# Register reads moved behind stores, two products moved inside a chain, one index tile split in five

## The chip, the cores and the metric

The kernel runs on one core of a Trainium2 chip, as one launch. The metric is the device time in microseconds (us) of that launch. TensorE (PE; its weight loads are shown apart as PEld) multiplies matrices, VectorE (DVE) and ScalarE (ACT) work elementwise, GpSimd (POOL) does elementwise work too and issues the indirect DMAs, SyncE (SP) issues most of the plain DMAs and reads numbers into registers. Each engine works through its own list in order; semaphores order the engines among themselves. 16 DMA engines move the data.

## What is computed

An attention block without softmax feeds a mixture of experts. With 8 batches, 8 heads, 576 positions and a head width of 64:

```python
kv = np.einsum('bhsd,bhse->bhde', k, v)
out = np.einsum('bhsd,bhde->bhse', q, kv)
rms = np.sqrt(np.mean(out * out, axis=-1, keepdims=True) + 1e-06)
x = (out / rms * g_norm)          # then (B,H,S,D) -> (4608, 512)

do_compute = x @ w_skip > 0
xc = x[do_compute]
logits = xc @ w_gate
e_idx = np.argmax(logits, axis=1)                      # 8 experts
probs = softmax(logits);  gate_w = probs[rows, e_idx]
for e in range(8):
    mask = e_idx == e
    h = np.maximum(xc[mask] @ w1[e], 0.0)              # 512 -> 1024
    y[mask] = gate_w[mask, None] * (h @ w2[e])         # 1024 -> 512
out = x.copy();  out[do_compute] = xc + y
```

Each token is 512 wide. A token with a score of zero or less keeps its x; every other one goes through the one expert that its logits choose.

## The kernel before

**Attention.** The 4608 tokens are worked in 36 units (`NU` = 36), two for each of 18 pairs of token tiles. A unit `n` runs in a loop over steps (L1034): `values(n)` on TensorE, `squares` on VectorE, `root` on ScalarE, `norm(n - 1)` on VectorE, then `weigh`, which puts the product with `g_norm` on a list `late`. `scale` works that list off; its job is `eng.tensor_tensor` at L628, on POOL unless an engine is named. A pair's x stands in a tile `xb` of two units; the pool `xb_pool` has six buffers, and pairs 2 to 5 stand in `room`, the space of a weight tile. When a pair's second product is issued, its two stores of 256 KB each (L670, or L659 for the last tile column of four batches, as in pair 17) are put down for the "end" part of a later step and issued by SP. All x is written to the output tensor `out` in DRAM; the experts' inputs are then gathered from there by row.

**The number chain.** For each group of token tiles `choose` finds the expert, `rank` counts on TensorE, and `number` (L724) turns ranks into slots on VectorE, in steps that are separated by `yield`: `pr` and `top`, `s_i`, `lo_i`, `hi_k` (the first four steps), then `oha_k`, a one-hot matrix, in pieces. `columns` (`hits` at L759, then `weighed` at L767) makes the other factor `bv`, and `place` (L779) multiplies both on TensorE so that each slot receives its token's row number. For the last group all of this runs at step `NU`, without a loop around it (L1054 to L1064). After `rank(LAST)` comes the whole of `number(LAST)`, then `columns`, and behind them `scale(NU, eng=nc.vector)`: the last two products, those of pair 17, on VectorE. POOL has taken the product ahead of them (L1059).

**SP's list.** `know_expert(r)` (L830) reads the number of the expert at place r into an SP register. For r = 1 to 7 this is put down for the "end" of step `NU - 1`. The stores of pairs 16 and 17 are put down for the "end" of step `NU + 1`, so they stand behind these reads.

**From rows to gathers.** Behind the loop, the first part of expert 0 (192 slots, gathered early) goes through layer 1 and layer 2 while the remaining rows are being found. After `place`, `add_pieces` adds the row numbers to `srow` (L837). `slot_rows` makes `rows` and `src`, the indices of whole pieces of 128 slots. Pieces that do not stand at a multiple of 128, or are shorter, need their rows moved over partitions. There are nine of these, in five runs of equal form, and `again_rows` makes `arows` and `asrc` for them: copies on ScalarE into `moved` (L1139), then two VectorE instructions a run (L1154, L1156). The first call makes two runs (`SOON = 2`), the second, after `first_1(range(6, 7))`, the other three. `first_1` is layer 1 on TensorE with its ReLU on ScalarE (L1201). Then `gather_all` issues the gathers of experts 0, 1 and 2 on POOL (L1171), each with `src` or `asrc` as its index. TensorE turns expert 0's two remaining pieces (L1180) as soon as they have landed, and the next load of weights (L341, L351) is tied to the last of these transposes.

The code of the last step, as it stands before:

```python
drain(choose(LAST))
scale(NU, chosen[-1], 2)
first_bv = weighed(known_at[0][:, :, :], 0, NE, row_k, 2, gat_pool, NE)
rank(LAST)
drain(number(LAST))
last_bv.append(columns(NE, NT - NE, colid_i, row_k, 2, gat_pool, NE))
scale(NU, eng=nc.vector)
```

Of the kernel before, what the change touches and what calls it, by code (L numbers as in the profile page):

```python
# [8 lines left out]
FP32 = mybir.dt.float32  # L9
BF16 = mybir.dt.bfloat16  # L10
I32 = mybir.dt.int32
# [6 lines left out]
def kernel(  # L18
# [43 lines left out]
    nc = tc.nc  # L62
    B, H, S, D = q.shape
    DM = H * D
    N = B * S
    P = 128
    C = S // 64
# [6 lines left out]
    E, F = moe_w1.shape[0], moe_w1.shape[2]  # L74
# [3 lines left out]
    FC = F // 128  # L78
# [17 lines left out]
    gat_pool = ctx.enter_context(tc.tile_pool(name="gat", bufs=1))  # L96
    ps_g = ctx.enter_context(tc.tile_pool(name="ps_g", bufs=1, space=bass.MemoryType.PSUM))
    attn = ctx.enter_context(ExitStack())
    kv_pool = attn.enter_context(tc.tile_pool(name="kv", bufs=3))
# [107 lines left out]
    for i in range(KVD):  # L207
        t = kvd_pool.tile([P, 2, 2, 2, PK], FP32, name=f"kvd{i}")
# [25 lines left out]
    for a in range(2):  # L234
        r = slice(a * 64, (a + 1) * 64)
        nc.vector.tensor_scalar(out=gw_b[r, :, a, :, :],
                                in0=wraw[r, :, :].rearrange("e n (u w) -> e u w n", u=2),
# [55 lines left out]
    runs = {}  # L293
    for r, off, m in sorted(res, key=lambda x: (x[0] > 0, x[1] < KEPT, x[0])):
        col = r * CK + off // P
# [18 lines left out]
    NRES = len(res)  # L314
# [110 lines left out]
    nq = 0  # L425
# [25 lines left out]
    def at(step, part, job):  # L451
        todo.setdefault((step, part), []).append(job)

    def jobs(step, part):
        for job in todo.pop((step, part), []):
            job()
# [161 lines left out]
    def weigh(n, xl):  # L618

        nq, b, i, u = units[n]  # L620
        if u == 0:
            if nq in IN_ROOM:
                x = room[:, IN_ROOM.index(nq) * 2 * DM:(IN_ROOM.index(nq) + 1) * 2 * DM]
                xbs[nq] = x.rearrange("p (r d) -> p r d", r=2)
            else:
                xbs[nq] = xb_pool.tile([P, 2, DM], FP32, tag="xb", name="xb")
        xb = xbs[nq]
        late.append((lambda eng: eng.tensor_tensor(  # L628
            out=xb[:, :, 4 * u * D:(4 * u + 4) * D].rearrange("p r (w x) -> p r w x", w=2),
            in0=xl[:, :, :, G:G + 2 * D] if i is None else  # L630
            xl[:, :, :, G:G + 2 * D].rearrange("p w r x -> p r w x"),
            in1=g_b[:, :, :].rearrange("p a d -> p (a d)").unsqueeze(1).unsqueeze(1)
                .to_broadcast([P, 2, 2, 2 * D]), op=ALU.mult), nq, u == 1 and (lambda: store_x(nq, b, i))))
# [7 lines left out]
    def scale(n, behind=None, keep=0, eng=None):  # L641

        while len(late) > keep:
            job, nq, store = late.pop(0)
            ins = job(eng or nc.gpsimd)
            if behind:
                tc.add_manual_dep(ins.ins, behind.ins.name, WAIT, reason="VectorE's port is free then")
            store = store() if store else None
            if store:
                at(max(min(n + 2, NU + 1), store_from.get(nq, 0)), "end", store)  # L650
# [73 lines left out]
    def number(g):  # L724

        t0, t1 = ([0] + ends)[g], ends[g]
        nt = t1 - t0
        ohb, rk = ohbs.pop(g), rks.pop(g)
        pr = gat_pool.tile([P, TG, E], FP32, tag="pr", name="pr")[:, 0:nt, :]
        nc.vector.tensor_tensor(out=pr, in0=rk[:, 0:nt, :], in1=ohb, op=ALU.mult)  # L730
        nc.vector.tensor_copy(out=top[:, :], in_=rk[:, nt, :])
        yield
        s_i = gat_pool.tile([P, TG], I32, tag="s_i", name="s_i")[:, 0:nt]
        with nc.allow_low_precision(reason="whole numbers"):
            nc.vector.tensor_reduce(out=s_i, in_=pr, axis=AX.X, op=ALU.add)
        yield
        lo_i = gat_pool.tile([P, TG], I32, tag="lo_i", name="lo_i")[:, 0:nt]
        nc.vector.tensor_single_scalar(out=lo_i, in_=s_i, scalar=127, op=ALU.bitwise_and)
        yield
        nc.vector.tensor_single_scalar(out=hi_k[:, t0:t1], in_=s_i, scalar=7,  # L740
                                       op=ALU.arith_shift_right)
        yield
        step = 2 if g < LAST else nt // 2
        for t in range(0, nt, step):
            nc.vector.tensor_tensor(out=oha_k[:, t0 + t:t0 + t + step, :],
                                    in0=row128_i[:, :].unsqueeze(1).to_broadcast([P, step, P]),
                                    in1=lo_i[:, t:t + step].unsqueeze(2).to_broadcast([P, step, P]),
                                    op=ALU.is_equal)
            yield

    def drain(pieces):
        for _ in pieces:
            pass
# [76 lines left out]
    def know_expert(r):  # L830
        experts_of.append(nc.values_load(
            order_i[0:1, r:r + 1], engines=(mybir.EngineType.SP,), min_val=0, max_val=E - 1,
            skip_runtime_bounds_check_because="a permutation of the experts"))
# [186 lines left out]
    streams, turned_ahead = [], []  # L1020
    now = [0]
    at(NU - 4, "pe", lambda: load_second(0, gathered[-1]))
    for r in range(1, E):
        at(NU - 1, "end", lambda r=r: know_expert(r))
    at(NU - 3, "early", lambda: first_in(0))
    at(NU - 2, "early", lambda: first_layer_1(range(1), slice(0, P)))
    at(NU - 2, "pe", lambda: first_in(1))
# [6 lines left out]
    for n in range(NU + 2):  # L1034
        now[0] = n
        if 1 <= n < NU - 1 and n + 1 not in turned_ahead:
            turn(n + 1)
        if 1 <= n < THIRD + 3 or n == NU:
            root(n - 1)
        jobs(n, "early")  # L1040
        if n < NU:
            values(n)
        jobs(n, "mid")
        if THIRD + 3 <= n < NU:
            squares(n)
        jobs(n, "summed")
        done = norm(n - 1) if 1 <= n <= NU else None
        if n < THIRD + 3:
            squares(n)
        jobs(n, "squared")  # L1050
        jobs(n, "pe")
        if done:
            done()
        if n == NU:  # L1054
            for pair, job in enumerate(last_x):
                job()
                first_hidden(pair)
            drain(choose(LAST))
            scale(NU, chosen[-1], 2)  # L1059
            first_bv = weighed(known_at[0][:, :, :], 0, NE, row_k, 2, gat_pool, NE)  # L1060
            rank(LAST)
            drain(number(LAST))
            last_bv.append(columns(NE, NT - NE, colid_i, row_k, 2, gat_pool, NE))
            scale(NU, eng=nc.vector)  # L1064
        jobs(n, "dve")

        if n in ends[:LAST]:
            streams.append((PACE[ends.index(n)], gating(ends.index(n))))
        for pace, stream in streams:
            for job in itertools.islice(stream, pace):  # L1070
                if job:
                    part, job = job if isinstance(job, tuple) else ("pe", job)
                    at(n + 1, part, job)
                    break
        jobs(n, "end")
    for _, stream in streams:
        assert next(stream, 0) == 0
    assert not todo
# [3 lines left out]
    with tc.tile_pool(name="wpool_b", bufs=1, reuse_waits="tile") as wpool_b, \  # L1082
# [60 lines left out]
        def again_rows(rows, src, which):  # L1143

            moved = gat_pool.tile([P, NRES], FP32, tag=f"moved{which.start}", name="moved")
            again_of(moved, srow, which)
            i = 0
            for j, ((_, m, _), cols) in enumerate(runs.items()):
                n = P // m
                cs = slice(i, i + len(cols))  # L1150
                i += len(cols)
                if j not in which:
                    continue
                nc.vector.tensor_scalar(out=rows[:, cs], in0=moved[:, cs], scalar1=float(n),  # L1154
                                        scalar2=part_of[m][:, 0:1], op0=ALU.mult, op1=ALU.add)
                nc.vector.scalar_tensor_tensor(out=src[:, cs], in0=rows[:, cs], scalar=N * n,  # L1156
                                               in1=rows[:, cs], op0=ALU.is_lt, op1=ALU.mult)


# [7 lines left out]
        whole = [[(c * P, P, r * CK + c, False) for c in range(CK)] for r in range(E)]  # L1167
        def gather_piece(xg, piece, src, asrc):
            off, m, col, aside = piece
            idx = asrc if aside else src  # L1170
            nc.gpsimd.indirect_dma_start(  # L1171
                out=x_of(xg, off, m), out_offset=None, in_=cut_rows(m)[:, :],
                in_offset=bass.IndirectOffsetOnAxis(ap=idx[:, col:col + 1], axis=0))

        def expert_in(xg, xt, piece):
            off, m = piece[0:2]
# [379 lines left out]
        def first_1(fs):  # L1556
            layer_1(0, xt_first, ht0, slice(0, KEPT), fs)
# [7 lines left out]
        add_pieces(srow[:, :], sp, 2)  # L1565
        y_more = layer_2(0, ht_of, first[1], None, range(IN))
        arows = gat_pool.tile([P, NRES], I32, tag="arows", name="arows")
        asrc = gat_pool.tile([P, NRES], I32, tag="asrc", name="asrc")
        again_rows(arows, asrc, range(0, SOON))
        rows, src = slot_rows(slice(0, NCOL), gat_pool, "")  # L1570
        first_1(range(6, 7))
        again_rows(arows, asrc, range(SOON, len(runs)))
        first_1(range(7, FC))
        for r in range(3):
            gather_all(r, plan, src, asrc)
        layer_2(0, ht_of, first[0], y, range(IN, FC))
# [78 lines left out]
```

## Time and profile before

| | us |
|---|---|
| median of 3 runs | 367.91 |
| lowest and highest run | 367.71, 371.33 |
| the profiled execution, its own time | 368.03 |
| its span from first to last instruction | 366.2 |
| PE busy | 349.9 (96% of the span) |
| DVE, ACT, POOL busy | 248.0, 147.6, 124.2 |

The profiled execution's time is 1.8 us above its span; this is what lies ahead of its first and behind its last recorded instruction. The granted TensorE clock was 0.993 of full speed over the span. DMA moved 81.70 MB, 223 GB/s in the mean.

The attention stage takes the first 108 us or so, with the DMA engines full from 20 to 80 us. From 140 us on eight experts run on a full TensorE. The change lies between the two. A row of a timeline is to be read as: start in us from the span's start, duration in us, engine, line, operation, what it writes and reads, how often, and in brackets the idle time of its engine ahead of it with what ended that. SPq and POOLq are an engine's sequencer, which issues DMAs and waits. "Issue" in a chain is time in which nothing shown was waited for.

### The profile page before, as it was taken

The numbers are of one execution on the slowest core, as the hardware profiler recorded it, in microseconds if no ns is written. First come the engines' busy times: TensorE is split into PE (matmuls) and PEld (weight loads), VectorE is DVE, ScalarE is ACT, GpSimd is POOL, SyncE is SP. The second block draws the span as 40 slices with busy tenths as digits, with TensorE's granted clock in tenths as the row PEclk, the third lists the DMA queues.
The fourth block names the chain that finished last, engine by engine and source line by source line (L and its number), as shares of the span: only waits on it lengthen the run. The fifth ranks groups of instructions, "written<-read, shape, count | busy, mean of one in ns | idle before, by whom it ended". The sixth has DMA issues, their size and how long they took to land.

```text
span 366.2 us, 9553 instructions
## 1 busy us (share of the span) xinstructions
PE 349.9 (96%) x3751; PEld 304.9 (83%) x3751; DVE 248.0 (68%) x630; ACT 147.6 (40%) x424; POOL 124.2 (34%) x201
## 2 busy tenths in 40 slices
PE   8979997999989999999999999999999999999993
PEld 4768886888878659599879988989988998989982
DVE  2646578678999653875937676786776776878831
ACT  2537675477775243335104402511431430431410
POOL 8037677567785072223032103303203203002002
PEclk9999999899999999999999999999999999999999
DMA  7999999999939659983536437465563762601001
GB/s 265 379 387 377 391 390 389 394 366 313 330 109 358 228 159 377 378 267 77 220 89 224 138 152 232 135 230 162 186 230 93 257 230 51 243 1 57 3 2 54
DMA packets 32808, 81.70 MB, mean 223 GB/s; under 512 B 3242, under 2 KB 3250, under 8 KB 32756
## 3 DMA queue, kind: packets, MB, share of 16 engines
q1 hardware_dynamic: 29264, 70.53, 54.3%
q0 software_dynamic: 3472, 10.48, 8.6%
q8 instruction: 31, 0.51, 0.6%
q14 instruction: 21, 0.17, 0.1%
q10 hardware_dynamic: 20, 0.02, 0.0%
HBM read 66.80 MB, written 14.48 MB: 222 GB/s over the span
## 4 chain that ended last, share of the span: by engine, by line
PE 74%; DMA 9%; issue 7%; DVE 3%; ACT 3%; POOL 2%; SPq 0%; POOLq 0%; DVEq 0%; ACTq 0%
PE bank L1279 45%; PE bank L1211 8%; PE o_ps L507 5%; DMA v<-in_v_dram 4%; PE sum_ps L387 4%; PE bank L1199 3%; PE q_ps L469 3%; DMA w<-in_moe_w_dram 2%; PE bank L1180 2%; DVE xl L554 1%; DMA out_dram<-xb 1%; DMA xg<-out_dram,src 1%; DMA xg<-out_dram,asrc 1%; DVE rs L531 1%; ACT qT L472 1%
## 5 line engine op out<-in xcount | busy, mean ns | idle before, releaser
L1289 ACT COPY p<-bank 128x128 f32<-128x128 f32 (+6 forms) x70 | 20.8, 297 | 96.3 <-PE bank L1279 88.8
L1279 PE MATMUL bank<-xt,w 128*128 128x128 f32 (+5 forms) x336 | 55.5, 288 | 0.0
L1410 POOL DMA_INDIRECT out_dram<-xg,rows x14 | 14.0, 997 | 117.6 <-DVE xg L1407 114.3
L1279 PEld LDWEIGHTS bank<-xt,w 128*128 128x128 f32 x336 | 47.0, 190 | 1.9 <-DVE bank L1283 1.4
L1283 DVE TENSOR_TENSOR bank<-bank,p 128x128 f32<-128x128 f32 (+6 forms) x70 | 23.6, 337 | 29.8 <-PE bank L1279 27.7
L628 POOL TENSOR_TENSOR xb<-xl,g_b 128x512 f32<-128x512 f32 x26 | 31.8, 1222 | 17.2 <-DVE rs L545 14.2
L1279 PE MATMUL bank<-xs,s 128*128 128x128 f32 (+5 forms) x224 | 36.7, 289 | 0.0
L507 PE MATMUL o_ps<-kvd,qT 128*128 128x146 f32 x240 | 35.7, 291 | 0.7 <-DVE xl L554 0.5
L507 PEld LDWEIGHTS o_ps<-kvd,qT 128*128 128x128 f32 x240 | 32.0, 192 | 1.6 <-DVE xl L554 1.1
L1279 PEld LDWEIGHTS bank<-xs,s 128*128 128x128 f32 x224 | 31.1, 190 | 1.0 <-ACT p L1289 0.8
L1211 PE MATMUL bank<-w,ht 128*32 128x128 f32 (+2 forms) x424 | 29.9, 313 | 0.0
L387 PE MATMUL sum_ps<-v,k 64*64 64x64 f32 x1152 | 24.4, 225 | 5.1 <-issue 4.4
L531 DVE TENSOR_REDUCE rs<-sq 128x8 f32<-128x512 f32 x36 | 24.5, 681 | 5.2 <-ACT sq L521 5.0
L387 PEld LDWEIGHTS sum_ps<-v,k 64*64 64x64 f32 x1152 | 20.2, 136 | 9.4 <-issue 6.4
L554 DVE TENSOR_TENSOR xl<-o_ps,rs 128x584 f32<-128x584 f32 x32 | 24.5, 767 | 3.9
L1211 PEld LDWEIGHTS bank<-w,ht 128*32 128x32 f32 (+2 forms) x424 | 18.2, 119 | 10.6 <-issue 7.2
L1279 PE MATMUL bank<-t,ht 128*128 128x256 f32 x112 | 27.0, 384 | 0.0
L1279 PE MATMUL bank<-w,ht 128*128 128x256 f32 x112 | 26.5, 380 | 0.0
L1171 POOL DMA_INDIRECT xg<-out_dram,src x14 | 14.5, 1034 | 33.4 <-DMA out_dram<-xg,rows 17.5
L1279 PE MATMUL bank<-t,hs 128*128 128x256 f32 x112 | 25.3, 379 | 0.0
L521 ACT ACTIVATE sq<-o_ps 128x512 f32<-128x512 f32 x34 | 20.3, 596 | 12.3 <-PE o_ps L507 10.0
L1279 PEld LDWEIGHTS bank<-t,ht 128*128 128x128 f32 x112 | 20.8, 190 | 3.9 <-issue 1.2
(217 smaller groups left out, 673.0 us busy)
## 6 DMA issues: line engine op xcount, KB each, us to landing
w<-in_moe_w_dram SPq DMA_DIRECT2D x16, 2048.0 KB, 10.5
k<-in_k_dram SPq DMA_DIRECT2D x32, 288.0 KB, 6.1
v<-in_v_dram SPq DMA_DIRECT2D x32, 288.0 KB, 6.1
q<-in_q_dram SPq DMA_DIRECT2D x32, 288.0 KB, 5.7
out_dram<-xb SPq DMA_DIRECT2D x25, 256.0 KB, 5.9
out_dram<-w SPq DMA_DIRECT2D x8, 256.0 KB, 4.7
out_dram<-xb POOLq DMA_DIRECT2D x3, 256.0 KB, 6.3
xg<-out_dram,src POOLq DMA_INDIRECT x16, 3.5
```

The lines of the kernel that those rows point to most:

```text
L387: nc.tensor.matmul(out=sum_ps[w * 64:(w + 1) * 64, a, u, :], lhsT=kt[r, 2 * u + w, c, :], rhs=vt[r, 2 * u + w, c, :], start=(c == 0), stop ...
L507: nc.tensor.matmul(out=ps[:, w, 0:2 * PK].rearrange("p (r k) -> p r k", r=2)[:, :, cols], lhsT=qT[:, w, a, :], rhs=kvds[b % KVD][:, w, :, ...
L521: nc.scalar.activation(out=sq[:, :, :, :], in_=heads(ps, G, G + 2 * D), func=ACT.Square)
L531: nc.vector.tensor_reduce(out=rs[:, :, :], in_=sq[:, :, :, :].rearrange("p x y (a d) -> p x (y a) d", a=2), axis=AX.X, op=ALU.add)
L554: nc.vector.tensor_tensor(out=xl[:, :, :, :].rearrange("p x y (a k) -> p x (y a) k", a=2), in0=ps[:, :, 0:2 * PK].rearrange("p x (h k) -> ...
L628: late.append((lambda eng: eng.tensor_tensor(out=xb[:, :, 4 * u * D:(4 * u + 4) * D].rearrange("p r (w x) -> p r w x", w=2), in0=xl[:, :, ...
L1171: nc.gpsimd.indirect_dma_start(out=x_of(xg, off, m), out_offset=None, in_=cut_rows(m)[:, :], in_offset=bass.IndirectOffsetOnAxis(ap=idx[:, ...
L1211: nc.tensor.matmul(out=yps[q * m:(q + 1) * m, 0:n], lhsT=ht(f)[:, off:off + m], rhs=w_sb[r][1][:, f, q * n:(q + 1) * n], start=(f == 0), s ...
L1279: nc.tensor.matmul(out=out, lhsT=lhsT(i), rhs=rhs(i), start=start and i == 0, stop=i == k - 1, skip_group_check=True)
L1283: nc.vector.tensor_tensor(out=to, in0=x, in1=y, op=ALU.add)
L1289: nc.scalar.copy(out=t, in_=x)
L1410: ins = nc.gpsimd.indirect_dma_start(out=cut_rows(m)[:, :], out_offset=bass.IndirectOffsetOnAxis(ap=rows[:, col:col + 1], axis=0), in_=x, ...
```

## The change

Four edits, all between the last steps of attention and the first gathers:

- `know_expert(1)` to `know_expert(7)` leave the "end" of step `NU - 1` and stand behind the whole loop, so behind all x stores on SP.
- The two products of pair 17 on VectorE leave their place behind `columns` and stand inside `number(LAST)`, behind `hi_k` and ahead of `oha_k`. Their output leaves `xb_pool` and takes a buffer of the pool that held K (three buffers in turn; this one was last used for batch 5).
- `asrc`, one tile of nine columns, becomes five tiles, one a run; each gather reads the column of its own run's tile.
- The second `again_rows` no longer stands between `first_1` of blocks 6 and 7 but ahead of both.

```diff
@@ weigh
                 xbs[nq] = x.rearrange("p (r d) -> p r d", r=2)
+            elif n >= NU - 2:
+                x = kv_pool.tile([P, 4, C, D], FP32, tag="k", name="k")
+                x = x[:, :, :, :].rearrange("p j c d -> p (j c d)")[:, 0:2 * DM]
+                xbs[nq] = x.rearrange("p (r d) -> p r d", r=2)
             else:
                 xbs[nq] = xb_pool.tile([P, 2, DM], FP32, tag="xb", name="xb")
@@ ahead of the loop
-    for r in range(1, E):
-        at(NU - 1, "end", lambda r=r: know_expert(r))
@@ step NU
             rank(LAST)
-            drain(number(LAST))
+            numbers = number(LAST)
+            for _ in range(4):
+                next(numbers)
+            scale(NU, eng=nc.vector)
+            drain(numbers)
             last_bv.append(columns(NE, NT - NE, colid_i, row_k, 2, gat_pool, NE))
-            scale(NU, eng=nc.vector)
@@ behind the loop
+    for r in range(1, E):
+        know_expert(r)
@@ again_rows
-                nc.vector.scalar_tensor_tensor(out=src[:, cs], in0=rows[:, cs], scalar=N * n,
+                nc.vector.scalar_tensor_tensor(out=src[j][:, :], in0=rows[:, cs], scalar=N * n,
                                                in1=rows[:, cs], op0=ALU.is_lt, op1=ALU.mult)
@@ gather_piece
-            idx = asrc if aside else src
+            at_row = asrc[col] if aside else src[:, col:col + 1]
             nc.gpsimd.indirect_dma_start(
                 out=x_of(xg, off, m), out_offset=None, in_=cut_rows(m)[:, :],
-                in_offset=bass.IndirectOffsetOnAxis(ap=idx[:, col:col + 1], axis=0))
+                in_offset=bass.IndirectOffsetOnAxis(ap=at_row, axis=0))
@@ ahead of the gathers
-        asrc = gat_pool.tile([P, NRES], I32, tag="asrc", name="asrc")
-        again_rows(arows, asrc, range(0, SOON))
+        asrcs = [gat_pool.tile([P, len(cols)], I32, tag=f"asrc{j}", name="asrc")
+                 for j, cols in enumerate(runs.values())]
+        asrc = [t[:, i:i + 1] for t, cols in zip(asrcs, runs.values()) for i in range(len(cols))]
+        again_rows(arows, asrcs, range(0, SOON))
         rows, src = slot_rows(slice(0, NCOL), gat_pool, "")
-        first_1(range(6, 7))
-        again_rows(arows, asrc, range(SOON, len(runs)))
-        first_1(range(7, FC))
+        again_rows(arows, asrcs, range(SOON, len(runs)))
+        first_1(range(6, FC))
```

## The prediction

> **What bounds the kernel now.** I read the head of the page first, then the busy times of each engine by stretch, then the chain of work that ended last, then the timeline of each engine between 115 and 136 us.
>
> ```profile
> PE 349.9 (96%) x3751; PEld 304.9 (83%) x3751; DVE 248.0 (68%) x630; ACT 147.6 (40%) x424; POOL 124.2 (34%) x201
> 131.50:133.40 1.90, 1.03 (x8) 0.66 (x9) 1.69 (x8) 0.59 (x1) 1.60 (x2) 1.00 0.38 71
> 140.00:150.00 10.00, 10.00 (x95) 7.78 (x97) 4.85 (x10) 5.48 (x22) 2.22 (x2) 1.00 1.03 385
> 240.00:366.00 126.00, 120.52 (x934) 110.25 (x932) 85.06 (x202) 34.13 (x101) 18.91 (x20) 0.99 0.37 127
> ```
>
> The last three rows are stretches: their length, then the busy time of PE, PEld, DVE, ACT and POOL, the granted clock, the DMA share and GB/s. TensorE is busy 96% of the span. In the expert stage it is simply full (10.00 of 10.00 us), so a microsecond saved ahead of 140 us reaches the end, and a microsecond saved on another engine inside that stage does not. The change touches only what happens between 116 and 134 us, and there one stretch is not full: 1.03 of 1.90 us. Whatever the change can bring is in these 0.87 us or close to them. The idle time in the last row lies at the end of the program, behind the last matmul, and moves with it.
>
> ```profile
> 119.46 3.60 PE L1211 MATMUL bank<-w,xg 128*128 128x512 f32 x8
> 122.90 0.51 PE L779 MATMUL g_ps<-bv,oha_k 128*128 128x48 bf16 x14
> 125.22 2.87 PE L1199 MATMUL bank<-xt_first,w 128*128 128x192 f32 x16
> 127.92 3.60 PE L1211 MATMUL bank<-w,ht 128*128 128x512 f32 x8
> 132.12 0.66 PE L1180 MATMUL bank<-ident,xg 128*128 128x128 f32 x4 [0.60 <-DMA xg<-out_dram,asrc]
> 133.04 0.33 PE L1180 MATMUL bank<-ident,xg 128*128 128x128 f32 x1 [0.27 <-DMA xg<-out_dram,asrc]
> 133.30 1.95 PE L1211 MATMUL bank<-w,ht 128*64 128x256 f32 x16
> ```
>
> The timeline of PE (start, duration, what, idle time before it and who ended it) shows the two gaps: 0.60 us and 0.27 us, each ended by the landing of a gather that reads its rows through `asrc`. They are the two pieces of expert 0 that are turned on TensorE at L1180. Every other instruction in this list starts where its predecessor ends. The chain says why these gathers are late:
>
> ```profile
> 123.70 4.17 DMA out_dram<-xb
> ...
> 128.75 1.00 POOL xg L1171
> 129.75 0.30 issue
> 130.06 2.94 DMA xg<-out_dram,asrc
> ```
>
> The last x store lands at 127.87 (123.70 + 4.17), the first gather starts at 128.75, the second at 130.06, and that lands at 133.00. The first gather has a second condition, which the timeline of POOL names:
>
> ```profile
> 128.75 1.00 POOL L1171 DMA_INDIRECT xg<-out_dram,asrc  x1 [10.82 <-DVE asrc L1156]
> 128.29 0.16 DVE L1156 SCALAR_TENSOR_TENSOR asrc<-arows 128x2 int32<-128x2 int32 x1
> DMA to landing us min/median/max: 2.9/3.1/3.3
> L1211 PE MATMUL bank<-w,ht 128*128 128x512 f32 x8 | 3.6, 592 | 0.0
> ```
>
> It waits for an index write that ends at 128.45, 0.58 us behind the last store. So two conditions end almost together, and both must move before the gather can. (The third line is the issue-to-landing time of the two gathers; the fourth, of the groups by form, gives the 592 ns of one of the eight matmuls from 127.92, which the sum uses.)
>
> **The change, part by part.**
>
> *Expert numbers behind the stores.* The timeline of the SP queue and the one line that groups the seven reads:
>
> ```profile
> 117.28 1.72 SPq L670 DMA_DIRECT2D out_dram<-xb  x2
> L831 SPq TENSOR_LOAD <-order_i x7: 262/273/530, 119.0 to 121.4; - x7
> 121.78 1.11 SPq L670 DMA_DIRECT2D out_dram<-xb  x2
> 123.02 1.50 SPq L659 DMA_DIRECT2D out_dram<-xb  x2
> 133.40 0.40 SPq L341 DMA_DIRECT2D w<-in_moe_w_dram  x1
> ```
>
> SP issues the stores of pair 15, then reads seven numbers from 119.0 to about 121.7, then issues the stores of pairs 16 and 17. The reads leave that place: 121.78 − 119.00 = 2.8 us. Pair 16's last product is POOL's, done at 117.80 (next fence), so its two stores can be issued from 119.0 and end near 120.15 (1.11 us). The reads now stand behind pair 17's stores, and the next thing behind them on SP is the weight load of expert 1, which goes out behind the transposes, at 133.40; seven reads of about 0.3 us from 121.7 end near 124, nine microseconds early. Cost nothing; cover, that wait.
>
> *The last products earlier.* VectorE's and POOL's timeline:
>
> ```profile
> 115.67 2.13 POOL L628 TENSOR_TENSOR xb<-xl,g_b 128x512 f32<-128x512 f32 x1 [2.87 <-DVE ohb L702]
> 117.28 0.67 DVE L738 TENSOR_SCALAR lo_i<-s_i 128x14 int32<-128x14 int32 x1
> 117.75 0.22 DVE L740 TENSOR_SCALAR hi_k<-s_i 128x14 int32<-128x14 int32 x1
> 117.99 2.10 DVE L745 TENSOR_TENSOR oha_k<-row_i,lo_i 128x896 bf16<-128x896 int32 x2
> 120.61 0.86 DVE L767 TENSOR_TENSOR bv<-ohc,row_k 128x672 bf16<-128x672 bf16 x1
> 121.38 1.29 DVE L628 TENSOR_TENSOR xb<-xl,g_b 128x512 f32<-128x512 f32 x2
> 123.45 0.39 DVE L837 TENSOR_TENSOR srow<-srow,g_ps 128x24 f32<-128x24 f32 x2 [0.78 <-PE g_ps L779]
> 124.55 0.16 DVE L1156 SCALAR_TENSOR_TENSOR asrc<-arows 128x1 int32<-128x1 int32 x1
> ```
>
> The two products (1.29 us) now start behind `hi_k`, at 117.99, and end at 119.28 instead of 122.67. Everything behind them in the chain moves by 1.29: `oha_k` ends near 121.4, `bv` at 122.76 instead of 121.47. `bv` is wanted by the 14 matmuls that start at 122.90, where TensorE is busy until that moment with the eight matmuls from 119.46. So 1.43 us of cover stand against 1.29 of delay: I cost it at nothing, with 0.14 us left. If that cover is gone, each microsecond of it is a microsecond of the program. The chain behind 123.45 then stands where it stood.
>
> *The free buffer.* The products write the buffer of K of an old batch, whose last reader is the state product of batch 5, far back. The `xb` slot that pair 17 had taken is freed by the stores of pair 11. The products did not wait for it: they start where `bv` ends. Moved ahead by 3.4 us they might have; bounds: 0 to 3.4 us of wait avoided. I take it that the buffer makes the start at 117.99 possible and adds nothing. Later owner of the space: weights of expert 1, loaded at 133, behind these stores anyhow.
>
> *The stores of pair 17* are issued when SP is free, 120.2, and take 1.50 for both; the second is issued at 120.9 instead of 123.70. Is DMA free to take them?
>
> ```profile
> 116.50:121.50 5.00, 5.00 (x43) 3.85 (x42) 4.84 (x11) 1.34 (x5) 1.42 (x2) 1.00 1.00 403
> 121.50:123.00 1.50, 1.50 (x8) 0.58 (x7) 1.17 (x2) 0.00 (x0) 0.00 (x0) 1.00 0.20 66
> 123.00:127.00 4.00, 4.00 (x42) 3.14 (x40) 1.57 (x9) 1.31 (x7) 0.00 (x0) 1.00 0.85 250
> ```
>
> The 16 DMA engines are full until 121.5 with earlier stores (403 GB/s), all but idle for 1.5 us while SP has been reading numbers, then move the last four stores, 1 MB, in 4 us. That idle stretch closes. From the issue: 120.9 + 4.17 = 125.1. From the engines: 1 MB behind 121.5 at 403 GB/s takes 2.6 us, 124.1 with nothing for the landing; at the 250 GB/s of the last row 4.2 us, 125.7. I take 125.3: 2.6 us earlier than 127.87.
>
> *Index tiles and the order on ScalarE.*
>
> ```profile
> 123.88 1.21 ACT L1139 COPY moved<-srow 64x1 f32<-64x1 f32 x6 [3.88 <-DVE srow L837]
> 126.82 0.33 ACT L1201 ACTIVATE ht<-bank 128x192 f32<-128x192 f32 x1 [1.74 <-PE bank L1199]
> 127.18 1.65 ACT L1139 COPY moved<-srow 64x1 f32<-64x1 f32 x8
> ```
>
> The eight copies no longer stand behind the ReLU at 126.82, which waits for TensorE, but directly behind the six copies that end at 125.09. They run 125.09 to 126.74, 2.1 us earlier, and the ReLU starts where it did. The late index writes come 2.1 us earlier, 126.36 instead of 128.45. With a tile for each run the first gather needs only the first run's, written at 124.71. So its conditions are 125.3 (store) and 124.71 or at worst 126.36 (index): start near 125.6, at worst 126.7, instead of 128.75. Five small tiles in place of one add no write and no gather.
>
> *Sum.* The gathers land near 128.9 and 129.9 (at worst 130.0 and 131.0). TensorE wants the first when its eight matmuls are done: they take 3.60 with the last one's end modelled at 0.59 us, so start follows start at 0.43 and the next can start at 131.36; four transposes at 0.11 ((0.66 − 0.33) / 3) and a fifth, then 0.26 to the following group (133.30 − 133.04), which starts at 132.06 instead of 133.30. That is 1.24 us; by the idle times alone it is 0.87. I take 1.1, between them, as starts are recorded and ends modelled. The slack of 1.9 us in the second gather means that errors in the stores' landing cost nothing until they pass it. Against the profiled execution's 368.03 us: 366.9; it lies 0.12 above the median of 367.91, so 366.8.
>
> **Where a page speaks against it.** The POOL product at 115.67 took 2.13 us while VectorE worked beside it, and `lo_i`, a thing of 14 columns, took 0.67 and ended 0.15 behind that product, against 0.22 for `hi_k`: VectorE stood behind POOL there. [...] By these rows POOL's last product ends at 117.80, before the product starts, so the sum stays; the case where they meet is the second rival.
>
> **Rivals.**
>
> *The gathers start no earlier.* Both conditions must move; if an index write of the last runs, or a wait of the stores' own semaphores, still holds the first gather to 128.75, the two gaps stay: 367.9. For it: two conditions within 0.6 us of each other now. Against it: 1.9 us of slack on one side and a shorter order on ScalarE on the other. Chance 0.10.
>
> *The number chain holds up TensorE.* Place: the 14 matmuls at 122.90. If the products meet POOL's and are held by one of its length, the chain moves by 1.29 + 2.13 = 3.42, the matmuls start 2.0 us late, and 2.0 − 1.1 leaves 0.9 lost: 368.8. It decides at 2.5 us for both products together (1.43 + 1.1), against 1.29 measured. Chance 0.05.
>
> *More is gained:* nothing else waits before 140 us on what moves; 0.03, about 366.
>
> **How the numbers follow.** My forecast, 366.8, has 0.82; alone it would be 366.3 to 367.3 (1.24 and 0.87 saved, with some scatter). The range takes in the first rival and part of the second and ends at 368.4; below, 366.0. About 1% (3.7 us) is what a measurement of this kernel can tell from no change. No case here reaches that by itself, neither 0.9 lost nor 1.24 gained: faster 0.02, same 0.95, slower 0.03.
>
> **What would show it.** Right: the reads of L831 behind the stores of L659; the last store landed by 126; the first gather at 125 to 127; no idle time before L1180 on PE; the group of 133.30 starting near 132.1. Wrong: idle time of PE before L779 at 122.9 (the chain), a DMA share still near 0.2 after 121.5 (the reads were not the reason), or the first gather still released by a late index write.

## The result

| | before | after |
|---|---|---|
| median of 22 runs each, us | 368.52 | 366.00 |
| lowest to highest, us | 365.98 to 373.9 | 363.52 to 367.96 |
| profiled execution: time, span, us | 368.03, 366.2 | 367.38, 365.6 |

The ratio is 0.9931, with a 95% interval of 0.9907 to 0.9954: 2.5 us less (1.7 to 3.4), which is within 1%. The 22 runs of before have a median 0.6 us above that of the three that were shown first. Ratios, and the comparisons at equal clock below, leave out runs that are more than 1.5% above the fastest of their kernel (in the experiments 11 of 211, 9 of them with the reads ahead of the stores). The two profiled executions differ by only 0.65 us, since the second one came later to the place of the change. A place in the program that both have is needed to compare them: the first matmul of the last rank group (`g_ps<-top`), in the timeline of PE, first before, then after.

```profile
115.20 0.48 PE L713 MATMUL g_ps<-top,ident 128*128 128x120 f32 x2 [0.66 <-ACT xg L881]
```

```profile
115.86 0.48 PE L717 MATMUL g_ps<-top,ident 128*128 128x120 f32 x2 [0.64 <-ACT xg L885]
...
123.56 0.52 PE L783 MATMUL g_ps<-bv,oha_k 128*128 128x48 bf16 x14
125.88 2.87 PE L1206 MATMUL bank<-xt_first,w 128*128 128x192 f32 x16
128.59 3.60 PE L1218 MATMUL bank<-w,ht 128*128 128x512 f32 x8
132.02 0.71 PE L1187 MATMUL bank<-ident,xg 128*128 128x128 f32 x5
132.66 1.95 PE L1218 MATMUL bank<-w,ht 128*64 128x256 f32 x16
```

The five transposes (L1180 before, L1187 after) now stand in one row with nothing in brackets, where there were two rows with 0.60 and 0.27 us of idle time. Called "the stage" from here on: from the rank matmul to the group behind the transposes. It took 133.30 − 115.20 = 18.10 us before and takes 132.66 − 115.86 = 16.80 after. The chain of the profile after passes through it on TensorE alone, with no transfer in it:

```profile
125.95 2.80 PE bank L1206 x16
128.75 3.43 PE bank L1218 x8
132.18 0.55 PE bank L1187 x5
132.73 1.88 PE bank L1218 x16
```

SP's queue and the stretches (length; PE, PEld, DVE, ACT, POOL; clock, DMA share, GB/s) show the order that was expected:

```profile
116.89 4.26 SPq L674 DMA_DIRECT2D out_dram<-xb  x5
121.25 1.42 SPq L663 DMA_DIRECT2D out_dram<-k  x2
L835 SPq TENSOR_LOAD <-order_i x7: 267/273/595, 122.7 to 125.2; - x7
```

```profile
117.50:122.00 4.50, 4.50 (x41) 3.48 (x40) 4.46 (x10) 0.98 (x3) 1.08 (x2) 1.00 1.03 415
122.00:123.50 1.50, 1.50 (x5) 0.51 (x4) 1.05 (x2) 0.00 (x0) 0.00 (x0) 1.00 0.98 395
```

The reads stand behind the stores, and where the DMA share had been 0.20 it is 0.98. VectorE and POOL:

```profile
116.33 2.13 POOL L632 TENSOR_TENSOR xb<-xl,g_b 128x512 f32<-128x512 f32 x1 [2.87 <-DVE ohb L706]
118.48 1.28 DVE L632 TENSOR_TENSOR k<-xl,g_b 128x512 f32<-128x512 f32 x2
122.29 0.86 DVE L771 TENSOR_TENSOR bv<-ohc,row_k 128x672 bf16<-128x672 bf16 x1
126.56 1.00 POOL L1178 DMA_INDIRECT xg<-out_dram,asrc  x1 [7.97 <-DVE src L850]
```

The products start at 118.48, `bv` is done at 123.15, and the first gather starts at 126.56: 10.70 us behind the rank matmul, where it had been 13.55.

### The profile page after: what moved, and what is told of

It is laid out like the page before. It is cut to its first block, busy times and chain, and to the rows that moved or that the text cites. A ratio compares the mean times of both kernels' runs of the same rounds, so it can differ in the third digit from the quotient of the medians.

```text
span 365.6 us, 9554 instructions
## 1 busy us (share of the span) xinstructions
PE 350.5 (96%) x3751; PEld 306.8 (84%) x3751; DVE 247.5 (68%) x630; ACT 147.4 (40%) x424; POOL 124.3 (34%) x201
## 4 chain that ended last, share of the span: by engine, by line
PE 79%; issue 7%; DMA 6%; DVE 3%; ACT 3%; POOL 1%; SPq 0%; POOLq 0%; DVEq 0%; ACTq 0%
PE bank L1286 45%; PE bank L1218 9%; PE o_ps L507 6%; PE sum_ps L387 4%; PE bank L1206 4%; PE q_ps L469 3%; DMA v<-in_v_dram 2%; DMA w<-in_moe_w_dram 2%; PE bank L1187 2%; DVE xl L554 1%; DMA xg<-out_dram,src 1%; PE o_ps L488 1%; PE g_ps L417 1%; PE g_ps L409 1%; DVE rs L531 1%
## 5 line engine op out<-in xcount | busy, mean ns | idle before, releaser
L1417 POOL DMA_INDIRECT out_dram<-xg,rows x14 | 14.0, 997 | 117.2 <-DVE xg L1414 114.0
L507 PE MATMUL o_ps<-kvd,qT 128*128 128x146 f32 x240 | 37.1, 299 | 0.7 <-DVE xl L554 0.5
L507 PEld LDWEIGHTS o_ps<-kvd,qT 128*128 128x128 f32 x240 | 33.3, 198 | 1.4 <-DVE xl L554 1.1
```

The source lines that it names most:

```text
L507: nc.tensor.matmul(out=ps[:, w, 0:2 * PK].rearrange("p (r k) -> p r k", r=2)[:, :, cols], lhsT=qT[:, w, a, :], rhs=kvds[b % KVD][:, w, :, ...
```

## The experiments

The question was why the runs gained 2.5 us where the stage of one pair of profiles shows 1.3, and which edit carries it. The table comes first; each kernel follows. "Stage" and "gather" (its first start behind the rank matmul) are from the profile of each kernel. "At equal clock" is the difference of the mean time to the before of the same chip and session, both brought to the same granted clock (how is told behind the experiments), with two standard errors. "Ahead" and "behind" say where the seven reads stand, against the stores of pairs 16 and 17.

| kernel | reads | ratio to before (95%) | at equal clock, us | stage, us | gather, us |
|---|---|---|---|---|---|
| before | ahead | | | 18.10 | 13.55 |
| before again | ahead | 0.9995 (0.9956–1.0033) | 0.0 ± 0.6 | 19.63 | 15.06 |
| before, tiles moved | ahead | 1.0032 (1.0002–1.0063) | −0.1 ± 0.6 | 17.66 | 12.83 |
| index edits alone | ahead | 1.0000 (0.9969–1.0031) | −0.6 ± 0.8 | 16.92 | 12.30 |
| change, reads put back | ahead | 0.9992 (0.9956–1.0029) | −0.3 ± 0.6 | 19.28 | 14.70 |
| before, two more profiles | ahead | | | 17.95, 18.03 | 13.35, 13.44 |
| reads alone | behind | 0.9952 (0.9922–0.9982) | −1.6 ± 0.7 | 17.02 | 12.35 |
| change, products late | behind | 0.9920 (0.9892–0.9947) | −1.6 ± 0.5 | 16.84 | 12.26 |
| change, old index | behind | 0.9955 (0.9923–0.9986) | −1.4 ± 0.6 | 16.80 | 10.64 |
| change, old buffer | behind | 0.9899 (0.9863–0.9934) | −2.7 ± 1.0 | 16.79 | 10.36 |
| change, old addresses | behind | 0.9924 (0.9892–0.9956) | −2.2 ± 0.8 | 16.80 | 11.37 |
| change again | behind | 0.9932 (0.9898–0.9966) | −2.1 ± 0.7 | 16.80 | 11.05 |
| the change | behind | 0.9931 (0.9907–0.9954) | | 16.80 | 10.70 |

**Is it the addresses?** The new tiles move other tiles in SBUF, and that might cost or save time anywhere. Four kernels: before once more, unedited; before with 96 more bytes ahead of `asrc`, so that tiles lie as after the change; the change with three small tiles put elsewhere, so that they lie as before; the change once more, unedited. The edits of the second and third:

```diff
         arows = gat_pool.tile([P, NRES], I32, tag="arows", name="arows")
+        space = gat_pool.tile([P, 24], I32, tag="space", name="space")
+        nc.gpsimd.memset(space[:, 0:1], 0)
```

```diff
-        key = gat_pool.tile([P, E], FP32, tag="key", name="key")
+        key = gat_pool.tile([P, TG], FP32, tag="fi", name="key")[:, 0:E]
...
-        at_r = gat_pool.tile([P, E], FP32, tag="at_r", name="at_r")
+        at_r = gat_pool.tile([P, TG], FP32, tag="mx", name="at_r")[:, 0:E]
...
-        rows = gat_pool.tile([P, 2], FP32, tag="rows1", name="rows1")
+        rows = gat_pool.tile([P, TG, E], FP32, tag="oh", name="rows1")[:, 0, 0:2]
```

> The kernel before, once more, for a second profile of it. Waits theory (the gain is the two gaps of TensorE ahead of the turned pieces, and other executions have larger gaps than the 0.87 us of the first profile): ratio 1.000; the gaps in this profile differ from 0.87 us, and the stage from the rank matmul (115.20 in the first profile) to the first matmul of the group at 133.30 takes more than the 18.10 us it took there, up to 20. Address theory (1.3 us from the gaps, the rest from SBUF addresses that the larger index tiles move by 96 bytes): gaps 0.9 again, stage 18.1.

> The kernel before with an unused tile of 96 bytes behind its index tiles, so that the tiles of attention and of the experts lie where the changed kernel has them. Waits theory: ratio 1.000 (0.998 to 1.002), since addresses do nothing. Address theory: ratio 0.996 to 0.997, 1.2 us less, and the time from the start to the rank matmul shorter than in the kernel before.

> The changed kernel with three small tiles of the number chain put into tiles that are free by then, which takes the 96 bytes back: attention and expert tiles lie where the kernel before has them. Waits theory: ratio 0.993, as the change. Address theory: ratio 0.9965, 1.3 us gained and no more.

> The changed kernel once more. Both: ratio 0.993 (0.990 to 0.996), no gap ahead of the turned pieces, 16.8 us from the rank matmul to the group behind them as in its first profile (115.86 to 132.66).

The first ran in 369.35 us, the second in 369.7, the third in 365.93, the fourth in 366.36 (medians). Before with the addresses of after is no faster, and the change with the addresses of before keeps its gain. The second ran 0.3% slower, and its granted clock was lower; at equal clock nothing of that is left (−0.1 ± 0.6). The theory of the addresses falls.

The unedited kernel brought something else. The same program, profiled again, has a gap of 2.18 us in place of 0.60 (timeline of PE):

```profile
116.98 0.48 PE L713 MATMUL g_ps<-top,ident 128*128 128x120 f32 x2 [0.57 <-ACT xg L881]
...
135.49 0.66 PE L1180 MATMUL bank<-ident,xg 128*128 128x128 f32 x4 [2.18 <-DMA xg<-out_dram,asrc]
136.36 0.33 PE L1180 MATMUL bank<-ident,xg 128*128 128x128 f32 x1 [0.21 <-DMA xg<-out_dram,asrc]
136.61 1.95 PE L1211 MATMUL bank<-w,ht 128*64 128x256 f32 x16
```

and its chain shows where that comes from: the last store takes 5.42 us to land, not 4.17.

```profile
125.75 5.42 DMA out_dram<-xb
```

So the 0.87 us in which the prediction looked for the whole gain are not a property of the kernel: they belong to one execution of it. The second kernel showed a further thing, in its timelines of POOL and VectorE:

```profile
128.09 1.00 POOL L1171 DMA_INDIRECT xg<-out_dram,asrc  x1 [10.06 <-DVE asrc L1156]
```

```profile
128.36 0.16 DVE L1156 SCALAR_TENSOR_TENSOR asrc<-arows 128x2 int32<-128x2 int32 x1
```

The first gather starts at 128.09, and the index write that the profile of before names as its releaser comes at 128.36, behind it. It cannot be a condition. What the gather does wait for shows when all fourteen traces are laid side by side: in thirteen of them it starts 0.87 or 0.88 us behind the landing of the last store (in before 127.87 and 128.75), wherever the index writes stand. The fourteenth is the kernel with the old buffer, below, and there it is the write of the first run's indices.

**Are the index edits worth anything?** The change with one index tile and the old order on ScalarE, and before with the index edits alone:

```diff
-        asrcs = [gat_pool.tile([P, len(cols)], I32, tag=f"asrc{j}", name="asrc")
-                 for j, cols in enumerate(runs.values())]
...
-        again_rows(arows, asrcs, range(SOON, len(runs)))
-        first_1(range(6, FC))
+        first_1(range(6, 7))
+        again_rows(arows, asrc, range(SOON, len(runs)))
+        first_1(range(7, FC))
```

> The change with its two index edits undone (one asrc tile, the second group of copies between blocks 6 and 7 of first_1). Stores theory (the first gather waits for the x stores alone; the late index write named in the profile before was not its condition): no gap ahead of the turned pieces, 16.8 us from the rank matmul to the group behind them, ratio 0.993. Two-conditions theory (as predicted: the index write at 128.45 holds the gather as much as the store): the first gather starts 13.3 us behind the rank matmul, as before, the gaps come back, ratio 0.997 to 1.000.

> The kernel before with the two index edits alone. Stores theory: nothing, ratio 1.000, 17.6 to 19.6 us from the rank matmul to the group. Two-conditions theory: a part of the gain where the stores landed early, the stage at most 17.8, ratio 0.997 to 0.999.

They ran in 366.41 and 368.76 us. The ratio of the first, 0.9955, lies between the two that were expected and does not decide by itself. Its profile does: it keeps a stage of 16.80 with all old index code, and in its timelines of POOL and VectorE the gather stands 2.45 us ahead of the late index write:

```profile
127.41 1.00 POOL L1178 DMA_INDIRECT xg<-out_dram,asrc  x1 [7.88 <-DVE rows L847]
```

```profile
129.86 0.16 DVE L1163 SCALAR_TENSOR_TENSOR asrc<-arows 128x2 int32<-128x2 int32 x1
```

The second brings nothing that its runs can tell. Its profile has a stage of 16.92, the shortest of any kernel with reads ahead, and its runs do not follow that profile. The row of its seven reads shows what was different in this execution:

```profile
L831 SPq TENSOR_LOAD <-order_i x7: 262/272/540, 116.0 to 118.4; - x7
118.75 1.11 SPq L670 DMA_DIRECT2D out_dram<-xb  x2
120.80 1.29 SPq L659 DMA_DIRECT2D out_dram<-xb  x2
```

The rank matmul starts at 113.31, so SP came to the reads 2.6 us behind it, where it was 3.8 in before, and the stores of pairs 16 and 17 followed at 5.4 and 7.5, where it was 6.6 and 7.8. Before with its tiles moved, which has the next shortest stage (17.66), came to its reads early too, at 1.1 us. So what the reads cost depends at least in part on when SP comes to them.

**Which edit carries the gain?** The change with the reads put back ahead of the stores; the change with the products back behind `columns`; before with the reads moved and nothing else.

```diff
@@ the change, reads put back
+    for r in range(1, E):
+        at(NU - 1, "end", lambda r=r: know_expert(r))
...
-    for r in range(1, E):
-        know_expert(r)
@@ the change, products late
-            numbers = number(LAST)
-            for _ in range(4):
-                next(numbers)
-            scale(NU, eng=nc.vector)
-            drain(numbers)
+            drain(number(LAST))
             last_bv.append(columns(NE, NT - NE, colid_i, row_k, 2, gat_pool, NE))
+            scale(NU, eng=nc.vector)
@@ before, reads alone
-    for r in range(1, E):
-        at(NU - 1, "end", lambda r=r: know_expert(r))
...
+    for r in range(1, E):
+        know_expert(r)
```

> The change with the seven register reads back at their old place, ahead of the stores of pairs 16 and 17; products and index edits as in the change. If the reads hold the stores: the stores of pair 17 are issued as late as before (7.8 us behind the rank matmul instead of 5.4), the gaps are back, ratio 1.000 (0.997 to 1.002). If the products held them: ratio 0.995 or less.

> The change with the two products of pair 17 back behind columns; reads and index edits as in the change. If the reads alone matter: ratio 0.993 and no gap. If both must move: pair 16's stores go out early, pair 17's wait for the products at 122.7 and go out 0.3 us earlier than in the kernel before; the DMA engines are freer then, so the last store lands 0.3 to 1 us earlier than before; gaps of 0.2 to 1 us, ratio 0.996 to 0.999.

> The kernel before with the register reads alone moved behind the stores; products, buffer and index tiles as before. If the reads alone carry the gain (as the run with the late products suggests): ratio 0.992 to 0.994, 16.8 to 17.0 us from the rank matmul to the group, last store landed 11.4 us behind the rank matmul. If the early products have a share: ratio 0.995 to 0.998, gaps of up to 1 us.

They ran in 367.97, 365.96 and 366.68 us. Without the move of the reads nothing is left of the gain, though products, buffer and index edits are all in; with the move alone, most of it is there. Of the two cases that were expected of the second, the one by which reads and products must both move fell. The chain of the first shows what the seven reads do on SP (four of its rows):

```profile
117.85 0.49 SPq L835
...
120.22 0.27 SPq L835
...
121.13 0.59 SPq L674
...
122.52 5.43 DMA out_dram<-k
```

Seven reads, from 117.85 to 120.48, then a store of pair 16, and the last store of pair 17 lands 5.43 us behind 122.52, at 127.95; the first gap on PE was 1.83 us. With the reads alone moved (rank matmul, transposes and the group behind them, cut off at 132 us; then the timeline of SP and the row that groups the reads):

```profile
114.02 0.48 PE L713 MATMUL g_ps<-top,ident 128*128 128x120 f32 x2
...
130.17 0.94 PE L1180 MATMUL bank<-ident,xg 128*128 128x128 f32 x5
131.04 1.30 PE L1211 MATMUL bank<-w,ht 128*64 128x256 f32 x10
```

```profile
115.79 3.21 SPq L670 DMA_DIRECT2D out_dram<-xb  x4
121.51 1.29 SPq L659 DMA_DIRECT2D out_dram<-xb  x2
```

```profile
L831 SPq TENSOR_LOAD <-order_i x7: 262/273/1073, 122.8 to 125.5; - x7
```

The stores of pair 16 go out without a stop, those of pair 17 at 121.51, when their late products are done: 7.5 us behind the rank matmul, against 5.4 in the change (121.25 − 115.86). The last store goes out only 0.3 us earlier than in before (8.17 us behind the rank matmul against 8.49), but with pair 16's stores ahead of it out of the way it lands 3.3 us later and not 4.2, at 11.47 against 12.67. No idle time stands ahead of the transposes, and the stage is 17.02, against 16.80 in the change. That is the price of late products with the reads behind, in one profile each: 0.2 us, and in the second kernel 0.04.

**Does the free buffer do anything?** The change without the branch in `weigh`, so that pair 17 takes its slot of `xb_pool` again:

```diff
-            elif n >= NU - 2:
-                x = kv_pool.tile([P, 4, C, D], FP32, tag="k", name="k")
-                x = x[:, :, :, :].rearrange("p j c d -> p (j c d)")[:, 0:2 * DM]
-                xbs[nq] = x.rearrange("p (r d) -> p r d", r=2)
```

> The change with pair 17's products in xb_pool as before instead of the free K buffer. If the buffer matters: the products, and oha_k and bv behind them, wait for the stores of pair 11 to land (2.6 us behind the rank matmul in the first profile of before, when the chain reaches them 2.6 behind it in the change), so up to 1 us of wait, eaten by the 0.2 us that bv has ahead of its matmuls, then TensorE late by the rest: ratio 0.993 to 0.997. If not: ratio 0.993, stage 16.8.

It ran in 365.13 us. Its products (timeline of VectorE, then its rank matmul) start 119.82 − 117.20 = 2.62 us behind the rank matmul, and those of the change 118.48 − 115.86 = 2.62. The slot was free.

```profile
119.82 1.28 DVE L628 TENSOR_TENSOR xb<-xl,g_b 128x512 f32<-128x512 f32 x2
```

```profile
117.20 0.48 PE L713 MATMUL g_ps<-top,ident 128*128 128x120 f32 x2 [0.26 <-ACT xg L881]
```

This execution also shows the gather's other condition. Its stores went out so early that the last one landed 1.89 us ahead of the first gather. The first run's index write, in the timeline of VectorE, ends at 126.71, and the gather starts 0.85 us behind it:

```profile
126.55 0.16 DVE L1159 SCALAR_TENSOR_TENSOR asrc<-arows 128x1 int32<-128x1 int32 x1
127.56 1.00 POOL L1174 DMA_INDIRECT xg<-out_dram,asrc  x1 [7.64 <-DVE asrc L1159]
```

**How often is the gap long?** Two more profiles of before, unedited.

> The kernel before, a look for the spread of its stage. Straggler theory (the stage is long when a 16 KB packet of the instruction queue runs ahead of the last store packets of one DMA engine, and that store then lands 1 to 1.5 us late): 17.5 to 18.1 us where the store's last packet ends before or as the 16 KB packet starts, 19 to 19.7 where it ends behind it. One-size theory: 17.7 to 18.1 wherever that packet lies.

> As the look before it: 17.5 to 18.1 us without, 19 to 19.7 us with the 16 KB packet ahead of the last store packets by the straggler theory; 17.7 to 18.1 in either case by the one-size theory.

They took 369.17 and 367.39 us, with stages of 17.95 and 18.03: neither shows the long case, so they only say that it is not the rule. In both the 16 KB packet begins as the store ends, where both theories allow such a stage, so the two are not told apart.

**What the stage accounts for.** The seven profiles with reads ahead have a stage of 18.22 us in the mean (16.92 to 19.63, standard error 0.35), the seven with reads behind 16.84 (16.79 to 17.02). The difference is 1.4 ± 0.7 us (two standard errors). All that follows the stage to the end of the span is the same in all fourteen: 232.93 to 233.08. What comes ahead of it differs, 113.3 to 117.2, in both kinds; it is there that the granted clock shows drops, for instance in the stretch from 60 to 80 us of before, and not of the change run again:

```profile
60.00:80.00 20.00, 18.05 (x375) 16.11 (x365) 13.67 (x32) 12.19 (x33) 12.79 (x23) 0.91 1.04 379
```

```profile
60.00:80.00 20.00, 16.91 (x363) 15.04 (x361) 13.63 (x31) 12.28 (x34) 12.87 (x24) 1.00 1.03 371
```

No profile has such a drop between 113 us and the last matmul; behind that one the clock falls again (0.84 from 362 to 366 us of before, 0.61 in the change), which costs nothing but counts in a mean. Each timed run lists the mean granted clock of its span, and so the two can be parted. Over the 200 executions of the three sessions of experiments (132 with reads ahead, 68 behind), fitted with a level for each session, the time falls by 2.8 us for each 0.01 of clock (standard error 0.2). Kernels with reads behind take 2.57 us less (standard error 0.21). At equal clock it is 1.85 us (0.16), and 0.7 us goes with a clock that is 0.0027 higher in the mean (0.9941 against 0.9914; standard error of the difference 0.0005). In executions with a clock of at least 0.997 the means are 367.45 (13 with reads ahead) and 365.31 (18 behind).

So 1.85 us of the gain are there at equal clock, which the stage's 1.4 ± 0.7 covers.

The 0.7 us that go with the clock are measured, and their cause is open, but the traces show what a drop of the clock is. Ahead of the last matmul it is either full or, for 3.41 us at a time, half. The fourteen traces have 13 such drops, none to two in a trace, seven in those with reads ahead and six in those with reads behind. Ahead of each, TensorE was busy for only 16 to 55% of a stretch of the same 3.41 us; in every other such stretch from 15 to 350 us (laid end to end, with the drops among them; the two drops of the change start 40.96 us apart, 12.00 such lengths) it was busy for 46% or more. The second profile of before has an example, and behind it the two stretches that its long gap of 2.18 us falls into (133.31 to 135.49), with the one that follows:

```profile
21.76:25.17 3.41, 1.45 (x32) 1.27 (x33) 0.85 (x3) 0.58 (x2) 0.65 (x2) 1.00 1.05 384
25.17:28.58 3.41, 3.41 (x18) 3.41 (x17) 1.95 (x4) 2.03 (x8) 2.63 (x7) 0.50 1.05 388
130.99:134.40 3.41, 2.31 (x6) 0.76 (x4) 1.59 (x6) 1.73 (x2) 1.96 (x2) 1.00 0.18 32
134.40:137.81 3.41, 2.11 (x17) 1.39 (x19) 3.24 (x7) 0.81 (x2) 2.60 (x3) 1.00 0.57 154
137.81:141.22 3.41, 3.41 (x29) 2.95 (x26) 0.23 (x1) 0.59 (x2) 2.50 (x4) 1.00 0.87 311
```

The gap is split, TensorE stays busy for 2.31 and 2.11 of 3.41 us (68 and 62%), and no drop follows. Inside one stretch the gap would have left 36% at most (1 − 2.18 / 3.41). So a long gap may cost a drop behind it in executions where it falls so, 1.7 us by half of 3.41 (an estimate), which the kernels with reads behind would be spared. No profile shows this case, and none shows that the idle time is the cause: it only comes ahead of the drops. A clock 0.0027 lower is about 0.6 of a drop an execution (0.0027 of 366 us, against 1.7), more than two long gaps in seven profiles suggest, so other reasons are not excluded.

The mean clock is also a rough measure, because it counts the fall behind the last matmul. If every drop cost its full 1.7 us, the clock's share would be 1.0 us in place of 0.7, and 1.6 us would be left at equal clock (an estimate).

## Why the prediction was off

*Bound and place: right as far as the profiles place the gain.* The idle time of the stage is gone, nothing behind the stage changed, and no other wait took the place of the one removed.

*The stores: right.* The last store was taken to land at 125.3, which is 10.1 us behind the rank matmul of before; by the trace's records of transfers it landed 9.85 behind it. The idle stretch of DMA closed, and the first gather came 10.70 behind the rank matmul where 10.4 (125.6) had been taken.

*The sum for this pair of profiles: near.* 1.24 by starts, 0.87 by idle times, 1.1 taken; 1.30 measured. Starts were the better measure.

*The step that failed* is the sentence "Whatever the change can bring is in these 0.87 us or close to them". It made the idle time of one execution the ceiling of the gain, so that the sum's saving came to 1.1 us. The runs gained 2.5. Of the 1.4 us above the ceiling, about 0.3 lie in the stage: over fourteen profiles it saves 1.4 ± 0.7. The two idle times together were 0.87 in the first profile, 2.39 in the next profile of the same program, 2.05 with the reads put back, and 0 to 0.8 in the others with reads ahead. The first profile was not an odd one among these (a stage of 18.10, mean 18.22). What it could not show is how far they scatter, nor anything outside the stage. About 0.4 us more is there at equal clock (1.85) and stands in no place that the profiles show, though the error of the stage's mean covers it. And 0.7 goes with the clock, for which the sum had no term and whose cause stays open. That the forecast of 366.8 was only 0.8 us off in the time itself is luck: the median of the three first runs, on which it stood, was 0.6 low. In the difference it gave 1.1 for 2.5.

*"Two conditions end almost together, and both must move": wrong.* The index write that the bracket of the POOL row named was no condition of the first gather (starts 0.27 and 2.45 us ahead of it in two runs); the last store's landing was, 0.87 us ahead of the start. The first run's index write is a true second condition, but in before it ended at 124.71, over 3 us ahead of that landing. The index tiles and the order on ScalarE were counted as half of the gain's conditions and are worth nothing that the runs can tell (−0.6 ± 0.8 us at equal clock). The first rival rested on the same sentence; its chance of 0.10 was too high for that reason.

*Products: harmless, as said, but of little use.* The chain has its cover: nothing idle ahead of L783, `bv` done 0.41 us ahead of it, where 0.14 had been counted. But with the reads behind the stores the products could have stayed: 0.04 and 0.2 us. The prediction saw that errors in the landing cost nothing until they pass the slack of the second gather, and did not use it here. By the table the stage is 16.8 as long as the first gather starts within some 12.2 us of the rank matmul, so the change has 1.5 us in hand, where 1.9 had been worked out; the late products use that up and no more.

*Reads at no cost, buffer adds nothing: right.* The reads end near 125.5, and the load behind them waits for the transposes; the products start 2.62 us behind the rank matmul with either buffer.

*POOL's product and VectorE:* the product took 2.13 us in both profiles, where the 33 ahead of it took 1.18 to 1.20, and `lo_i` beside it took 0.67, where its two earlier calls, with 12 and 10 columns and no product on POOL beside them, took 0.16 and 0.17. In the profile after, POOL's product ended at 118.46 and the first product on VectorE started at 118.48: they did not meet, and the sum stayed as it was. That a product on VectorE would be held by one of POOL's length, the 2.13 us of the second rival, no run shows.

*Rivals.* Gathers no earlier: fell, by 2.85 us. The number chain: fell. "More is gained", given 0.03 and 366: this is the time that came. It was named without a mechanism, and the reason against it, that nothing else waits before 140 us, looked at the stage of one profile. The runs place no more than a part of what came above 1.1, so the number was met without the mechanism.

## What to carry to other kernels

The gap that ended with the landing of a transfer was no constant here (0.60 us in one execution of before, 2.18 in the next), and one profile's idle time is not a ceiling of what the runs can gain: take a second and third profile of the same kernel, and compare runs at equal clock. In before, seven register reads kept SP's queue for 2.6 us, and the store behind them, whose data were ready at 117.80, went out at 121.78; on a queue that also issues stores, put such a read behind the last one if its reader is far off. And check a releaser that the profile names in other runs, above all where two ends lie within about half a microsecond of each other: a true one kept its distance to what it releases (here 0.87 or 0.88 us in thirteen traces), a false one did not (here it ended 0.3 us ahead of the start in before, and stood 0.27 and 2.45 us behind it in two other runs).

## What the runs showed of the hardware

- Seven reads of one number each took SP 2.6 us (0.26 to 0.53 us each in before), and the DMA share fell to 0.20 behind them.
- Restarted, the stores ran slower: by the trace's packet records the 128 packets of 4096 bytes of pair 16 took 268 to 280 ns (median) in the seven profiles in which they stand behind such a pause, and 159 ns in an unbroken stream, and the stretches give 250 against 395 to 415 GB/s. By these figures the pause cost more than its own length.
- From the landing of the last store to the start of the first gather it took 0.87 or 0.88 us in all thirteen traces in which that store came last.
- Ahead of the last matmul the granted clock was half for 3.41 us at a time, each time behind 3.41 us in which TensorE had been busy for 16 to 55%.
- The last store's time from issue to landing was 4.2 us in three of four profiles of before, 3.3 and 3.7 in two more kernels with reads ahead, 3.3 to 3.9 in the kernels with reads behind, and 5.4 in the two executions with the long gap. In those two a packet of 16,384 bytes of the instruction queue (about 0.93 us) begins while the last store is still moving. A thin rest of the store goes on as that packet ends (12.68 against 12.70 us behind the rank matmul, and 12.73 against 12.75) and ends 1.2 us later than the bulk. In six others such a packet begins as the store ends, and with the index edits alone it begins 0.17 us ahead of the store's end and that store is not late (3.3 us). That this packet holds up the store is inferred from two executions, of seven with reads ahead; the records do not say on which DMA engine it ran.
